# First mixture layer: where the unsplit fp32 rows of w2 come from, a load per buffer or a load per expert and a GpSimd copy per slot

## The chip, the cores and the metric

The kernel runs on one NeuronCore of a Trainium2 chip. The metric is the device time of one execution in microseconds. The median of three runs of the kernel before is 710.54 us (706.63 to 710.76). The execution that the profiler recorded took 707.83 us, of which 706.0 us are the span from its first to its last instruction.

## The reference

Attention with two kinds of window masks gives a matrix x of 2304 tokens by 512. Two mixture layers with 8 experts follow, and each token goes to one expert:

```
logits = x @ w_gate
e_idx = argmax(logits)
for e in range(8):
    h = relu(x[mask] @ w1[e])          # 512 x 1024
    ye = h @ w2[e]                     # 1024 x 512
    out[mask] = gate_w * eom * ye      # second layer: gate_w only
```

All arrays are fp32. An expert has 2 MB of w1 and 2 MB of w2.

## The kernel before

After the attention the tokens of each mixture layer are sorted by expert into slots of 128 rows, and the function `moe` works through the slots one after the other. In the first layer, the subject here, there are 23 slots (0 to 22) with these inputs. A slot is one pass of TensorE: 96 matmuls of 128 columns (L797) for x @ w1 in two halves of four hidden blocks, then 12 fp16 matmuls of 512 columns and 8 more, of which 4 are in fp32 (both L864), for h @ w2, and 12 small ones for the router of the next layer (L1017).

Weights are multiplied as a sum of two fp16 numbers, hi and lo. An expert's fp32 weights are loaded by DMA into `raw` (8 pieces of 128 x 1024, four of w1 and four of w2), ScalarE makes hi from them (L99) and VectorE makes lo (L104), both into one of two weight buffers, `wbuf[0]` and `wbuf[1]`, which alternate from slot to slot. The split is made anew for every slot. Its operations stand in strings: `B0:4` makes hi and lo of half pieces 0 to 4, `D0:4` loads the same half pieces of the slot after next into `raw`. The strings for a slot are `MO['ta1']`, which is `SQ4`; their four parts are issued at four places of the slot.

In this layer the last two pieces (half pieces 12 to 16, the last four blocks of w2) are not split: the last four matmuls of a slot multiply them in fp32 (`plain`, L77). `plains(s + 1)`, called at the start of slot s, loads these two pieces, 1 MB, by two DMAs straight into `wbuf[(s + 1) % 2]`.

SyncE (SP) issues all weight DMAs in order. Each is conditional: a register read from a table (`tab`, a value load, which is a TENSOR_LOAD and two register operations) says whether the expert of the slot is another one. `tab[:, 1]` says so against the slot before and steers the loads into `raw`; `tab[:, 2]` says so against the slot two before, which had the same buffer, and steers the loads into `wbuf`. With these inputs the experts have 3, 3, 2, 2, 3, 3, 4 and 3 slots, so the expert changes at slots 3, 6, 8, 10, 13, 16 and 20; the loads into `wbuf` move data for slots 3 and 4, 6 and 7, 8 and 9, 10 and 11, 13 and 14, 16 and 17, 20 and 21. In the other slots their instructions pass without moving data.

In a slot SP issues, in this order: `plains(s + 1)`; in slots 5 to 15 the loads of a part of the second layer's first expert (`Fill`, L930); two value loads; `D0:4`; the transpose of the last output rows for the router (`yT`, L1003) and their store (`y_dram`, L1004); the transposed gather of tokens (`xT`, L770); the other loads into `raw`. GpSimd (POOL) issues: the gather of tokens for slot s + 2 (L763); a copy of indices (L990); the lo part of the output rows (L998); in slots 6 to 16 the lo part of a fill (L940, L941).

Of the kernel before, what the change touches and what calls it, by code (L numbers as in the profile page):

```python
# [24 lines left out]
P = 128  # L25
# [12 lines left out]
SP4 = ['B0:4 D0:4', '', 'B4:6 D4:6', 'B6:8 D6:8 B8:12 D8:12 B12:14 D12:14 H14:16 L14:15 P15:16 D14:16']  # L38

UF = 12  # L40
SQ4 = ['B0:4 D0:4', '', 'B4:6 D4:6', 'B6:8 D6:8 B8:12 D8:12']
MO = {'ta1': SQ4, 'wm': 9, 'f': ['H0:2 H2:4 H4:6 H6:8 P0:2', 'L2:8', 'H14:16 H8:14 P14:16 L8:14'], 'rf': 18, 'yh': 1, 'ta': ['H0:4 L0:3 P3:4 D0:2', '', 'B4:6 D2:6', 'B6:8 D6:8 B8:12 D8:12 B12:14 D12:14 B14:16 D14:16'], 'tb': SP4,
      's3': ['B0:4 D0:4', 'B4:8 D4:8', 'B8:12 D8:12', ''], 's4': ['B0:4 D0:4', 'B4:8 D4:8', 'B8:12 D8:12 B12:14 D12:14 H14:16 L14:15 P15:16 D14:16']}
OOB = 1 << 20
ROW = 2 * DM + 16

# [2 lines left out]
def fused(ctx, tc, qk, vw, wr1, w1a, w2a, mid, wr2, mbias, w1b, w2b, cf, c16, cbs, cms, cib, out, dbg=None):  # L49
    nc = tc.nc  # L50
# [50 lines left out]
    def lo_piece(wb, k, n=2, pool=None):  # L101
        s = slice(k * 512, (k + n) * 512)
        if pool is None:
            nc.vector.scalar_tensor_tensor(out=wb[:, 1, s], in0=raw[:, s], scalar=SW, in1=wb[:, 0, s],  # L104
                                           op0=ALU.mult, op1=ALU.subtract)
        else:
            nc.gpsimd.tensor_scalar(pool[:, 0:n * 512], raw[:, s], SW, None, op0=ALU.mult)  # L107
            nc.gpsimd.tensor_tensor(wb[:, 1, s], pool[:, 0:n * 512], wb[:, 0, s], op=ALU.subtract)  # L108

    def splits(wb, ops, load=None):  # L110

        for o in ops.split():
# [478 lines left out]
    def sort(nm, lg, nt, inv, fe, ea, tab, scale, og, extra, gscale, start):  # L591
# [4 lines left out]
        T = work(nm, nt)  # L596
# [87 lines left out]
        v.tensor_scalar(sc, iota_t, nlast, -float(KA), op0=ALU.min, op1=ALU.add)  # L684
        cmp2 = T("cmp2", [NSLOT, E])
        v.tensor_tensor(cmp2, end.unsqueeze(1).to_broadcast([P, NSLOT, E]), sc.unsqueeze(2).to_broadcast([P, NSLOT, E]), op=ALU.is_le)
        ef = T("ef", [NSLOT + 2])
        v.memset(ef[:, 0:2], 0.0)
        v.tensor_reduce(out=ef[:, 2:], in_=cmp2, axis=AX.X, op=ALU.add)
        ei = T("ei", [NSLOT], I32)  # L690
        v.tensor_scalar(ei, ef[:, 2:], fe["g"], None, op0=ALU.add)
        v.tensor_tensor(tab[:, 1, 0:NSLOT], ef[:, 2:], ef[:, 1:NSLOT + 1], op=ALU.not_equal)
        v.tensor_tensor(tab[:, 2, 0:NSLOT], ef[:, 2:], ef[:, 0:NSLOT], op=ALU.not_equal)
        v.tensor_scalar(tab[:, 0, 0:NSLOT], ei, E - 1, None, op0=ALU.bitwise_and)
        eql = T("eql" + nm, [NSLOT])
        v.tensor_scalar(eql, iota_t, nlast, None, op0=ALU.is_equal)
# [520 lines left out]
```

## Time and profile before

| | |
|---|---|
| median of three runs | 710.54 us (706.63 to 710.76) |
| profiled execution | 707.83 us |
| its span | 706.0 us |
| mean granted TensorE clock | 0.946 of full speed |
| PE busy | 613.3 us (87%) |
| DVE busy | 523.3 us (74%) |
| ACT busy | 440.3 us (62%) |
| POOL busy | 394.5 us (56%) |
| moved by DMA | 133.72 MB |

PE is TensorE, DVE VectorE, ACT ScalarE. The attention takes about the first 160 us, the first mixture layer runs from 163.8 us to 468.5 us, the second to the end. The view of waits says who waited for whom, the timeline lists instructions with start, duration, and, in brackets, the idle time before them and what ended it. Times in all rows are microseconds from the start of the span, where not marked ns.

### The profile page before, as it was taken

What the parts mean: (1) busy time and instruction counts of PE and PEld (TensorE: products, weight loads), DVE (VectorE), ACT (ScalarE), POOL (GpSimd) and SP (SyncE); (2) the same over time, 40 slices, a digit from 0 to 9 for tenths busy, and PEclk for the clock granted to TensorE, in tenths of its full rate; (3) what the DMA queues carried; (4) which work ended last, traced back from release to release, by engine and by line L of the source; (5) the groups of instructions that cost most, each with busy time, mean ns of one, the idle gap of its engine ahead of it and who ended that gap; (6) DMA issues with size and microseconds to landing.
All of it is one profiled execution on the core that took longest, in us unless ns stands there. A gap on an engine that the chain in (4) does not pass through costs nothing. (4 is left out here: it accounts for less than half of the span.)

```text
span 706.0 us, 18711 instructions
## 1 busy us (share of the span) xinstructions
PE 613.3 (87%) x7180; PEld 458.7 (65%) x7180; DVE 523.3 (74%) x658; ACT 440.3 (62%) x529; POOL 394.5 (56%) x396
## 2 busy tenths in 40 slices
PE   3898879836989987999998979999799987999993
PEld 2788768725757664676675757676676764776771
DVE  4699887684349565686767845759399987999995
ACT  4687766531166556676757646731389866889883
POOL 2577675442472545576666832312679946756771
PEclk9999998857999998999999989999999998999997
DMA  9999999983687999998989589430953299323231
GB/s 203 231 228 241 244 242 251 266 239 90 163 232 164 301 238 275 339 252 263 274 244 253 133 209 259 103 65 17 291 85 105 77 306 289 58 68 92 61 78 47
DMA packets 134484, 133.72 MB, mean 189 GB/s; under 512 B 94447, under 2 KB 99311, under 8 KB 133360
## 3 DMA queue, kind: packets, MB, share of 16 engines
q1 hardware_dynamic: 128704, 114.56, 64.1%
q0 software_dynamic: 5280, 17.13, 8.2%
q8 instruction: 60, 0.98, 0.6%
q10 hardware_dynamic: 400, 0.72, 0.4%
q14 instruction: 40, 0.33, 0.1%
HBM read 209.91 MB, written 18.22 MB: 323 GB/s over the span
## 5 line engine op out<-in xcount | busy, mean ns | idle before, releaser
L104 DVE SCALAR_TENSOR_TENSOR wb<-raw,wb 128x1024 f16<-128x1024 f32 (+2 forms) x190 | 326.6, 1747 | 82.8 <-ACT wb L99 81.9
L99 ACT ACTIVATE wb<-raw 128x1024 f16<-128x1024 f32 (+1 forms) x190 | 256.9, 1399 | 69.1 <-DMA raw<-in_w1a 45.9
L797 PEld LDWEIGHTS <-wb 128*128 128x128 f16 x4032 | 232.8, 99 | 16.1 <-DMA xsA<-lotmp 6.7
L797 PE MATMUL ph<-xT,wb 128*128 128x128 f16 x3648 | 213.9, 221 | 3.7 <-DMA xT<-xg 3.7
L864 PE MATMUL py<-wb,hh 128*128 128x512 f16 x524 | 125.1, 392 | 16.0 <-ACT hh L808 16.0
L864 PE MATMUL py<-wb,hl 128*128 128x512 f32 (+1 forms) x304 | 112.4, 511 | 6.2 <-ACT hl L805 5.3
L864 PEld LDWEIGHTS <-hh 128*128 128x128 f16 x580 | 55.7, 100 | 79.7 <-ACT hh L808 17.4
L808 ACT ACTIVATE hh<-ph 128x512 f16<-128x512 f32 x61 | 36.3, 595 | 57.6 <-PE ph L797 39.6
L864 PEld LDWEIGHTS py<-wb,hl 128*128 128x128 f32 x168 | 32.9, 198 | 42.5 <-issue 32.3
L990 POOL COPY y<-idxaa 128x1 int32<-128x1 int32 x21 | 15.7, 745 | 74.2 <-DMA y_dram<-y 74.2
L107 POOL TENSOR_SCALAR lotmp<-raw 128x512 f32<-128x512 f32 x17 | 31.3, 1843 | 21.4 <-DMA raw<-in_w1b 20.1
L403 PE MATMUL po<-v,pT 128*96 128x65 f32 x384 | 41.4, 262 | 1.5 <-DMA v<-in_vw 1.5
L763 POOL DMA_INDIRECT xg<-x_dram,idxaa x23 | 37.4, 1628 | 8.3 <-DVE idxaa L669 4.2
L998 POOL TENSOR_TENSOR y<-y,y 128x512 f16<-128x512 f32 x21 | 31.9, 1519 | 17.5 <-ACT y L997 15.1
L108 POOL TENSOR_TENSOR wb<-lotmp,wb 128x512 f16<-128x512 f32 x17 | 29.6, 1743 | 18.3 <-issue 16.1
L403 PEld LDWEIGHTS po<-v,pT 128*96 128x96 f32 x384 | 38.2, 177 | 2.0 <-DMA v<-in_vw 1.6
L1109 POOL DMA_INDIRECT out<-y,idx x18 | 32.4, 1799 | 7.5 <-DMA raw<-in_w2b 4.7
L344 DVE TENSOR_REDUCE M<-ps 96x4 f32<-96x512 f32 x48 | 31.6, 678 | 3.4 <-PE ps L343 3.2
L301 DVE SCALAR_TENSOR_TENSOR kl<-qk,kh 128x608 f16<-128x608 f32 x32 | 29.2, 915 | 6.3 <-ACT kh L298 6.3
L809 DVE SCALAR_TENSOR_TENSOR hl<-ph,hh 128x512 f16<-128x512 f32 x38 | 25.7, 679 | 10.7 <-ACT hh L808 10.7
L342 PE MATMUL ps<-kh,qs 128*96 128x128 f16 x192 | 30.5, 234 | 3.0 <-ACT kh L298 2.9
L797 PE MATMUL ph<-xsA,wb 128*128 128x128 f16 x384 | 24.9, 229 | 8.2 <-DMA xsA<-lotmp 6.6
(358 smaller groups left out, 886.0 us busy)
## 6 DMA issues: line engine op xcount, KB each, us to landing
raw<-in_w1a SPq DMA_DIRECT2D x92, 512.0 KB
raw<-in_w1b SPq DMA_DIRECT2D x72, 512.0 KB
raw<-in_w2b SPq DMA_DIRECT2D x72, 512.0 KB
raw<-in_w2a SPq DMA_DIRECT2D x46, 512.0 KB
wb<-in_w2a SPq DMA_DIRECT2D x44, 512.0 KB
qk<-in_qk SPq DMA_DIRECT2D x16, 608.0 KB
v<-in_vw SPq DMA_DIRECT2D x16, 390.0 KB
y_dram<-y SPq DMA_DIRECT2D x21, 260.0 KB
```

Of the source, the lines that this page charges most:

```text
L99: nc.scalar.activation(wb[:, 0, s], raw[:, s], AF.Copy, scale=SW)
L104: nc.vector.scalar_tensor_tensor(out=wb[:, 1, s], in0=raw[:, s], scalar=SW, in1=wb[:, 0, s], op0=ALU.mult, op1=ALU.subtract)
L107: nc.gpsimd.tensor_scalar(pool[:, 0:n * 512], raw[:, s], SW, None, op0=ALU.mult)
L342: nc.tensor.matmul(ps[:, j, :], st, kh[:, h, QT * i:QT * i + 128], start=False, stop=False, skip_group_check=True)
L344: nc.vector.tensor_reduce(out=Ms[n][:, 4 * g:4 * g + 4], in_=ps, axis=AX.X, op=ALU.max)
L403: nc.tensor.matmul(po[:, i, :], pT[:, NQ * h + i, :], v[:, h, i, :], start=True, stop=True)
L763: nc.gpsimd.indirect_dma_start(t, None, src, bass.IndirectOffsetOnAxis(start.idx[:, s:s + 1], 0))
L797: nc.tensor.matmul(ph[:, j, :], w[:, c, fs], xT[:, parts[c + i], :], start=k == 0, stop=k == 47, skip_group_check=True)
L808: nc.scalar.activation(hs, ph, AF.Relu)
L864: nc.tensor.matmul(to, a, w, start=k == 0, stop=k == len(ops) - 1)
L998: gt.tensor_tensor(y16[:, DM:2 * DM], self.y, y16[:, 0:DM], op=ALU.subtract)
L1109: gt.indirect_dma_start(out, bass.IndirectOffsetOnAxis(idx2[:, s:s + 1] if s is not None else ilast, 0), y, None, bounds_check=N - 1, oob_ ...
```

## The change

The two unsplit pieces are now loaded into `raw`, as the other six are, by the same register as these: once for each expert. In every slot GpSimd copies them from there into the weight buffer of the next slot by two copies of 128 x 1024 fp32 (`C12:16`, issued behind `B8:12`). The third row of the table and its value load are gone.

```diff
-SQ4 = ['B0:4 D0:4', '', 'B4:6 D4:6', 'B6:8 D6:8 B8:12 D8:12']
+SQ4 = ['B0:4 D0:4', '', 'B4:6 D4:6', 'B6:8 D6:8 B8:12 C12:16 D8:12']
...
-      's3': ['B0:4 D0:4', 'B4:8 D4:8', 'B8:12 D8:12', ''], 's4': [...]}
+      's3': ['B0:4 D0:4', 'B4:8 D4:8', 'B8:12 D8:12', 'C12:16'], 's4': [...]}
...
+            if o[0] == "C":
+                for i in range(k // 2, e // 2):
+                    nc.gpsimd.tensor_copy(plain(wb)[i - UF // 2], raw[:, i * 1024:(i + 1) * 1024])
...
-        v.tensor_tensor(tab[:, 2, 0:NSLOT], ef[:, 2:], ef[:, 0:NSLOT], op=ALU.not_equal)
...
-            load_raw(w1, w2, regs[0], cond=regs[1], pieces=[k for k in pieces if k < npc])
+            load_raw(w1, w2, regs[0], cond=regs[1], pieces=[k for k in pieces if (k < npc) != rest])
...
         def plains(s):
 
-            if s < NSLOT and one:
-                c = None if s < KE + 2 else nc.sync.value_load(tab[0:1, 2, s:s + 1], min_val=0, max_val=1)
-                load_raw(w1, w2, evr.pop(s), cond=c, pieces=range(npc, 8), wb=wbuf[s % 2])
+            weights(s, always=s == KE, rest=True)
```

On POOL, in slot 7, the order before is this (`xg` is the gather, `idxaa` the table of token indices, `wb_2778` the buffer that the fill prepares for the second layer):

```order
L763 DMA xg_2779<-x_dram,idxaa 128x1024
L990 COPY y_2797<-idxaa 128x1
L998 TENSOR_TENSOR y_2797<-y_2801,y_2797 128x512
L940 TENSOR_SCALAR xgA_2783<-xgA_2783 128x512
L941 TENSOR_TENSOR wb_2778<-xgA_2783,wb_2778 128x512
```

and after the change:

```order
L766 DMA xg_2779<-x_dram,idxaa 128x1024
L990 COPY y_2797<-idxaa 128x1
L998 TENSOR_TENSOR y_2797<-y_2801,y_2797 128x512
L940 TENSOR_SCALAR xgA_2783<-xgA_2783 128x512
L941 TENSOR_TENSOR wb_2778<-xgA_2783,wb_2778 128x512
L123 COPY wb_69<-raw 128x1024 x2
```

The two copies come last in the slot, so they stand ahead of the gather, L990 and L998 of the next slot.

On SP, where slot 6 begins, the order before is this (`wb_2766` is `wbuf[1]`, the buffer of slot 7; the first row is the last load of `D8:12` of slot 5; `xgA` and `lotmp` are stages of the fill):

```order
L91 DMA raw<-in_w2a 128x2x512 [waits DMAHW6_49]
L786 TENSOR_LOAD tab_2787
L786 ISA x2
L91 ISA
L91 DMA wb_2766<-in_w2a 128x2x512 [waits DMAHW7_49,PE_49]
L91 ISA
L91 DMA wb_2766<-in_w2a 128x2x512 [waits DMAHW0_49,PE_49]
L930 ISA
L930 DMA xgA_2783<-in_w1b 128x512 [waits DMAHW1_49]
```

and after the change:

```order
L91 DMA raw<-in_w2a 128x2x512 [waits DMAHW6_49]
L91 ISA
L91 DMA raw<-in_w2a 128x2x512 [waits DMAHW7_49,Pool_49]
L91 ISA
L91 DMA raw<-in_w2a 128x2x512 [waits DMAHW0_49,Pool_49]
L930 ISA
L930 DMA xgA_2783<-in_w1b 128x512 [waits DMAHW1_49]
```

The value load is gone, the two loads have another target and another condition, and they wait for POOL (the copies of the slot before, which read `raw`) where they waited for PE.

## Rows read from the trace of the kernel before

**Rows 1.** Waits on all engines, 245 to 472 us: total, times, longest.
```profile
ACT wb L99 <- DMA raw<-in_w1a: 33.9, 10, 6.0
...
PE py L864 <- ACT hl L805: 5.3, 4, 2.2
PE py L864 <- ACT hh L808: 5.0, 4, 3.4
PE plg L1017 <- DMA yT<-y: 4.8, 2, 4.4
```

**Rows 2.** PE timeline, slots 7, 9, 10 and 11: start, duration, instruction.
```profile
266.56 4.45 PE L864 MATMUL py<-wb,hh 128*128 128x512 f16 x12 [3.38 <-ACT hh L808]
272.93 5.40 PE L864 MATMUL py<-wb,hl 128*128 128x512 f32 x8 [1.92 <-ACT hl L805]
...
299.12 3.70 PE L864 MATMUL py<-wb,hl 128*128 128x512 f32 x8 [0.85 <-ACT hl L805]
302.96 5.52 PE L797 MATMUL ph<-xT,wb 128*128 128x128 f16 x96
308.32 2.75 PE L864 MATMUL py<-wb,hh 128*128 128x512 f16 x12
310.91 3.60 PE L864 MATMUL py<-wb,hl 128*128 128x512 f32 x8
314.65 5.52 PE L797 MATMUL ph<-xT,wb 128*128 128x128 f16 x96
```

**Rows 3.** ACT timeline, slot 7.
```profile
261.75 1.91 ACT L99 ACTIVATE wb<-raw 128x2048 f16<-128x2048 f32 x1 [5.79 <-DMA raw<-in_w1a]
...
270.30 1.06 ACT L99 ACTIVATE wb<-raw 128x1024 f16<-128x1024 f32 x1 [3.79 <-DMA raw<-in_w1a]
```

**Rows 4.** SP timeline, slots 6, 8 and 11: the loads into wb and raw.
```profile
251.03 1.15 SPq L91 DMA_DIRECT2D wb<-in_w2a  x2
...
254.87 0.98 SPq L91 DMA_DIRECT2D raw<-in_w1a  x2
...
280.22 1.16 SPq L91 DMA_DIRECT2D wb<-in_w2a  x2
...
318.66 0.50 SPq L91 DMA_DIRECT2D wb<-in_w2a  x2
```

**Rows 5.** DMA rate, 250 to 260 us, in slices of 0.25 us.
```profile
GB/s 291 196 0 0 0 0 0 0 90 74 98 147 156 336 385 410 410 418 410 418 418 352 369 393 401 410 393 344 303 344 311 360 262 115 147 147 262 295 367 412
```

**Rows 6.** Line L786, the value load of the third table row: ns, minimum, median, maximum.
```profile
L786 SPq TENSOR_LOAD <-tab x19: 263/278/587, 221.8 to 457.2; - x19
```

**Rows 7.** POOL operations with one input: two casts (us, mean ns), and line L107 (ns).
```profile
L363 POOL CAST mb<-r 96x12 bf16<-96x12 f32 x16 | 3.0, 190 | 1.1
...
L499 POOL CAST identh<-cft 128x128 f16<-128x128 f32 x1 | 0.3, 290 | 0.0
...
L107 POOL TENSOR_SCALAR lotmp<-raw x17: 1487/1578/3439, 517.8 to 681.9; 128x512 f32<-128x512 f32 x17
```

**Rows 8.** Busy us of PE, PEld, DVE, ACT, POOL, then granted clock; sum over 251-390.
```profile
270.00:285.00 15.00, 13.08 (x125) 8.52 (x124) 10.04 (x8) 11.57 (x14) 9.52 (x6) 0.86 0.98 295
...
345.00:360.00 15.00, 15.00 (x142) 9.87 (x141) 12.08 (x11) 13.04 (x15) 13.72 (x8) 1.00 0.73 200
...
sum 139.00, PE 129.48 PEld 87.50 DVE 94.28 ACT 93.16 POOL 87.02; mean PE 14.39 PEld 9.72 DVE 10.47 ACT 10.35 POOL 9.67
```

**Rows 9.** DVE and POOL timelines, where the two overlap.
```profile
230.29 2.29 DVE L104 SCALAR_TENSOR_TENSOR wb<-raw,wb 128x2048 f16<-128x2048 f32 x1 [0.57 <-ACT wb L99]
...
230.40 2.30 POOL L180 TENSOR_SCALAR fe_ub<-fe_ob 128x8 f32<-128x8 f32 x1
...
308.92 2.37 POOL L940 TENSOR_SCALAR xgA<-xgA 128x512 f32<-128x512 f32 x1
...
310.30 1.23 DVE L104 SCALAR_TENSOR_TENSOR wb<-raw,wb 128x1024 f16<-128x1024 f32 x1 [0.36 <-ACT wb L99]
...
311.37 1.17 POOL L941 TENSOR_TENSOR wb<-xgA,wb 128x512 f16<-128x512 f32 x1
```

More of the change, by code (lines that the diff above doesn't have):

```diff
@@ L40 @@
 UF = 12
-SQ4 = ['B0:4 D0:4', '', 'B4:6 D4:6', 'B6:8 D6:8 B8:12 D8:12']
+SQ4 = ['B0:4 D0:4', '', 'B4:6 D4:6', 'B6:8 D6:8 B8:12 C12:16 D8:12']
 MO = {'ta1': SQ4, 'wm': 9, 'f': ['H0:2 H2:4 H4:6 H6:8 P0:2', 'L2:8', 'H14:16 H8:14 P14:16 L8:14'], 'rf': 18, 'yh': 1, 'ta': ['H0:4 L0:3 P3:4 D0:2', '', 'B4:6 D2:6', 'B6:8 D6:8 B8:12 D8:12 B12:14 D12:14 B14:16 D14:16'], 'tb': SP4,
-      's3': ['B0:4 D0:4', 'B4:8 D4:8', 'B8:12 D8:12', ''], 's4': ['B0:4 D0:4', 'B4:8 D4:8', 'B8:12 D8:12 B12:14 D12:14 H14:16 L14:15 P15:16 D14:16']}
+      's3': ['B0:4 D0:4', 'B4:8 D4:8', 'B8:12 D8:12', 'C12:16'], 's4': ['B0:4 D0:4', 'B4:8 D4:8', 'B8:12 D8:12 B12:14 D12:14 H14:16 L14:15 P15:16 D14:16']}
 OOB = 1 << 20
@@ L566, in fused @@
     xsb = [m1.tile([P, 8, P], F16, name=f"xT{i}") for i in range(3)]
-    tabs = [m1.tile([P, 3, 32], I32, name=f"tab{i}") for i in range(2)]
+    tabs = [m1.tile([P, 2, 32], I32, name=f"tab{i}") for i in range(2)]
     for t in tabs:
@@ L686, in sort @@
         v.tensor_tensor(cmp2, end.unsqueeze(1).to_broadcast([P, NSLOT, E]), sc.unsqueeze(2).to_broadcast([P, NSLOT, E]), op=ALU.is_le)
-        ef = T("ef", [NSLOT + 2])
-        v.memset(ef[:, 0:2], 0.0)
-        v.tensor_reduce(out=ef[:, 2:], in_=cmp2, axis=AX.X, op=ALU.add)
+        ef = T("ef", [NSLOT + 1])
+        v.memset(ef[:, 0:1], 0.0)
+        v.tensor_reduce(out=ef[:, 1:], in_=cmp2, axis=AX.X, op=ALU.add)
         ei = T("ei", [NSLOT], I32)
-        v.tensor_scalar(ei, ef[:, 2:], fe["g"], None, op0=ALU.add)
-        v.tensor_tensor(tab[:, 1, 0:NSLOT], ef[:, 2:], ef[:, 1:NSLOT + 1], op=ALU.not_equal)
-        v.tensor_tensor(tab[:, 2, 0:NSLOT], ef[:, 2:], ef[:, 0:NSLOT], op=ALU.not_equal)
+        v.tensor_scalar(ei, ef[:, 1:], fe["g"], None, op0=ALU.add)
+        v.tensor_tensor(tab[:, 1, 0:NSLOT], ef[:, 1:], ef[:, 0:NSLOT], op=ALU.not_equal)
         v.tensor_scalar(tab[:, 0, 0:NSLOT], ei, E - 1, None, op0=ALU.bitwise_and)
@@ L750, in moe @@
     def moe(w1, w2, tab, src, parts, post, start, wfirst):
-        xg, xs, regs, evr = {}, {i: xsA[i] for i in range(KA)}, [], {}
+        xg, xs, regs = {}, {i: xsA[i] for i in range(KA)}, []
         one = post is post1
@@ L772, in x_transpose, with weights @@
             post.gathered(s, g)
-        def weights(s, pieces=range(8), always=False):
+        def weights(s, pieces=range(8), always=False, rest=False):
             if s >= NSLOT:
@@ L779, in weights @@
                            None if always else nc.sync.value_load(tab[0:1, 1, s:s + 1], min_val=0, max_val=1), s)
-                evr[s] = regs[0]
-            load_raw(w1, w2, regs[0], cond=regs[1], pieces=[k for k in pieces if k < npc])
+            load_raw(w1, w2, regs[0], cond=regs[1], pieces=[k for k in pieces if (k < npc) != rest])
         def plains(s):
-            if s < NSLOT and one:
-                c = None if s < KE + 2 else nc.sync.value_load(tab[0:1, 2, s:s + 1], min_val=0, max_val=1)
-                load_raw(w1, w2, evr.pop(s), cond=c, pieces=range(npc, 8), wb=wbuf[s % 2])
+            weights(s, always=s == KE, rest=True)
         def mm1(g, w1h, w1l, xT, mid):
```

## The prediction, made before the changed kernel ran

> **What bounds the kernel now.** I read the view of waits first, then the PE timeline, then the queues behind its gaps. In the first mixture layer PE sets the pace: slot 10 begins at 302.96 and slot 11 at 314.65, so an undisturbed slot takes 11.69 us, and PE has no gap in it [rows 2]. What is lost stands beside this pace, and few waits carry it: between 245 and 472 us PE waits 5.0 us for hh, 5.3 us for hl and 4.8 us for yT, 15.1 us together [rows 1]. hh and hl are made by ScalarE, and ScalarE is not slow: in the same stretch it waits 33.9 us for the w1 pieces in `raw` [rows 1]. It works in order, so an hh that stands behind a split whose weights have not landed is late, and PE with it. The costliest place is slot 7: the split of slot 8's first pieces starts at 261.75 after 5.79 us of waiting, the next at 270.30 after 3.79 us [rows 3]; PE waits 3.38 us for hh and 1.92 us for hl, and its 12 and 8 matmuls take 4.45 and 5.40 us where slot 10 needs 2.75 and 3.60 [rows 2]. The granted clock of 270 to 285 us is 0.86, so part of the stretch ran at 1.2 instead of 2.4 GHz, after PE had stood idle [rows 8]. Slot 7 thus loses 5.30 us of waiting and 3.50 us of slow matmuls, 8.80 us. Slot 9 loses 0.85 us to hl [rows 2].
>
> The DMA queues cause this. The loads for slot 8 are issued at 254.87, and in front of them stand the 1 MB that `plains` loads into `wbuf` for slot 7, issued at 251.03 [rows 4], and two fills. From 253.5 to 256.5 us the rate is at 336 to 418 GB/s, about 400 [rows 5]: the queue is full, and what comes first delays what comes behind.
>
> **The change, part by part.**
>
> *Loads removed.* The expert changes at 7 slots. Before, each change moves 2 MB into the two buffers, now 1 MB into `raw`: 7 loads of 1 MB go, those for slots 4, 7, 9, 11, 14, 17 and 21. One takes 2 x 128 x 1024 x 4 B / 400 GB/s = 2.6 us of full queues, 18 us in all, but only what stands ahead of a late load counts.
> - The load for slot 7, at 251.03, stands ahead of the late one. Slot 8's pieces should land 2.6 us sooner, and the 3.38 us wait shrink to 0.8. The second wait, 1.92 us, is for the next piece, which shifts by as much; I leave it. Of the 1.70 us that the slow clock costs the 12 matmuls behind the first wait I take half, 0.85, since I can't tell whether 0.8 us of idling still lowers it. Bounds: 0 (the fills fill the gap) and 8.80 us. I take 3.45.
> - The load for slot 9, at 280.22 [rows 4], stands ahead of those for slot 10, which split late in slot 9: the 0.85 us wait should go. Bounds 0 and 0.85; I take 0.85.
> - The other five stand ahead of no late load of the same slot: the next expert comes three or more slots after each change, and its loads are issued a slot later, into queues that have drained. The waits that remain in [rows 1] after slots 7 and 9 (5.0 - 3.38, 5.3 - 1.92 - 0.85 and 4.8, together 8.95 us) belong to other slots. I take 0; bounds 0 and 8.95.
>
> *The value load.* SP saves one per slot, 0.28 us [rows 6], and pays three more in slot 2, where the register has been given to another slot in between. Below 1 us either way, off PE's path: 0.
>
> *Copies added.* Two copies of 128 x 1024 per slot on POOL, in 20 slots. The trace has no copy of this size. From the casts, 190 ns for 12 columns and 290 for 128 [rows 7], a column costs 0.86 ns, which makes 190 + 1012 x 0.86 = 1.06 us. From above, L107, also with one input, needs 1487 ns for 512 columns at the least [rows 7], so 2.97 us for 1024. I take 1.06, because the casts are the same kind of operation without arithmetic: 2.1 us per slot. POOL is busy 87.02 of 139 us, 7.3 us in 11.69 [rows 8], and 7.3 + 2.1 = 9.4 fits. What hides them: the buffer that they fill is read by the last four matmuls of the next slot, some 10 us later. They can't gain by themselves, since no instruction of POOL goes. I take 0; the price if the cover is gone is the slower rival below.
>
> *Waits added.* SP's loads at the start of a slot now wait for the copies of the slot before. Behind them on SP stand the fills, the loads of the next expert, yT, y_dram and xT; ScalarE and the router matmuls wait for these. In slot 10 the last fill operation on POOL ends at 311.37 + 1.17 = 312.54 [rows 9], the copies then at 314.7, and SP comes to that load at 318.66 [rows 4]: 4 us to spare. Behind the copies on POOL stand the gather, L990 and L998 of the next slot; SP's yT waits for L998. The gather is two slots ahead. I take 0.
>
> *VectorE against GpSimd.* At 230.40 an operation of 8 columns on POOL took 2.30 us, the length of the VectorE split that began at 230.29: it waited for it. But L940, on POOL from 308.92 to 311.29, did not keep the split at 310.30 from running its plain 1.23 us [rows 9]. So a copy may wait for a split of up to 2.29 us, and VectorE for less than a copy. VectorE is busy 94.28 of 139 us, 7.9 us per slot, and 7.9 + 2.1 is still under 11.69 [rows 8]; lo is made a slot ahead. 0.
> The Trainium skill ("SBUF — State Buffer", section "SBUF: two separate sides") calls the port pair of the two engines "an exclusive lock, not a bandwidth split", held for the whole instruction, also by a VectorE operation with two SBUF inputs. The first row agrees, the second does not. By that rule VectorE would lose the copies' full 2.1 us per slot, and in 345 to 360 us, where it is busy 12.08 of 15 us [rows 8], 9.4 + 2.1 = 11.5 us would leave it nothing to spare: the sum stays, the slower rival gains.
>
> *Sum.* 3.45 + 0.85 = 4.3 us. The profiled execution took 707.83 us, so 703.5. The median of the three runs is 2.7 us above the profiled execution; from it the same sum gives 706.2. I say 705.0, between the two.
>
> **Rivals.**
> 1. *Hidden anyway.* The fills and the transposes take the place of the removed megabyte, the pieces land when they did, and the copies cost nothing: 707.8 to 710.5, say 709. For it: in rows 5 the rate still reaches 412 GB/s at 260 us, long after the removed load. Against it: a queue in order must shorten by what leaves it. Chance 0.18.
> 2. *The whole of slot 7 goes.* SP itself is held by the full queues; if it runs ahead by 2.6 us the second piece is also issued sooner than it shifts, the clock stays up, and 8.80 + 0.85 us go, with half a microsecond at the yT wait of 4.4 us [rows 1]: 10.2 us, 697.6. For it: both waits have one cause. Against it: 3.79 us for the second piece is more than one megabyte. Chance 0.18.
> 3. *Slower: POOL becomes the bound.* A copy waits for a whole split, as the operation at 230.40 did, so 2 x (1.06 + 2.13) = 6.4 us per slot; at the price of L107 it is 5.9 without any wait. With 7.3 us of other work POOL needs 13.7 us, 2.0 over the slot's 11.69. It decides from 2.2 us per copy. L998, then yT and SP's loads come later from slot to slot. In the slots with fills that have no large wait of their own (8, 10 to 14 and 16, seven) this is 14 us, less the 4.3: 717.5. For it: POOL is busy 13.72 of 15 us from 345 to 360 us [rows 8]. Against it: much of that is itself waiting for VectorE. Chance 0.14.
>
> **How the numbers follow.** The forecast, 702 to 707, has a chance of 0.50. A measurement of this kernel tells about 1% (7 us) from no change. Faster by over 1% is rival 2 and a small part, 0.05, of the forecast: 0.23. Slower by over 1% is rival 3 but for 0.02 where POOL falls behind only a little: 0.12. Within 1%: 0.65. The range runs from 697, which takes in rival 2, to 715, which leaves out the bulk of rival 3: 697 to 715.
>
> **What would show it.** Right: in the profile after, `raw<-in_w2a` has as many issues as both targets had, with 7 MB less moved; slot 7's wait for hh is near 0.8 us; the copies take 1.1 us where VectorE is idle and up to 3.4 us behind a split; the undisturbed slots still take 11.69 us. Wrong: slots 10 to 14 get longer, SP waits for POOL at the loads into `raw`, or PE's wait in slot 7 is as long as before.

## The result and the profile after the change

The kernel got slower: 715.34 us median (712.37 to 718.13) against 709.39 us for the kernel before beside it, a ratio of 1.0092 with a 95% interval of 1.0062 to 1.0121. The prediction, 705.0 us, has the wrong sign, and the measured time lies 0.3 us above its range of 697 to 715. The profiled execution took 717.02 us, its span 715.2 us.

The page after the change: busy time of the engines, VectorE's split line and the copies.

```profile
PE 611.7 (86%) x7180; PEld 457.7 (64%) x7180; DVE 546.2 (76%) x656; ACT 440.0 (62%) x529; POOL 463.2 (65%) x438
...
L104 DVE SCALAR_TENSOR_TENSOR wb<-raw,wb 128x1024 f16<-128x1024 f32 (+2 forms) x190 | 349.2, 1870 | 69.0 <-ACT wb L99 64.2
...
L123 POOL COPY wb<-raw 128x1024 f32<-128x1024 f32 x42 | 72.0, 1735 | 16.4 <-DMA raw<-in_w2a 16.4
```

POOL has 72.0 us of copies, and VectorE 22.9 us more than the 523.3 us of before, though it was given no work. DMA moved 126.39 MB, the expected 7.3 MB less.

Where the time went is seen from slot lengths. I count a slot from one group of router matmuls to the next, and the layer from the first matmul of slot 0 to the group that ends slot 22 (one more group follows among the matmuls of the second layer):

```profile
167.29 2.95 PE L797 MATMUL ph<-xsA,wb 128*128 128x128 f16 x26 [6.65 <-DMA xsA<-lotmp]
...
478.13 0.45 PE L1017 MATMUL plg<-wr2h,yT 128*128 128x8 f16 x12
```

The layer (PE timeline, after) is 478.13 - 167.29 = 310.8 us long, against 468.5 - 163.8 = 304.7 before: 6.2 us. The other 3 us of the two profiled executions arise in the attention, which the change doesn't touch; over all the traces below the layer starts at 163.3 to 167.3. Slot lengths in us, for six kernels that are used below (slots not shown differ by less than 0.9, slot 8 by 1.2, slot 13 by 1.7, and slots 0 to 2 together by 1.6):

| slot | before | before again | after | before + constant copies | copies on ScalarE | no copies |
|---|---|---|---|---|---|---|
| 6 | 12.94 | 12.79 | 12.78 | 14.21 | 12.55 | 12.77 |
| 7 | 20.81 | 20.07 | 13.12 | 13.33 | 13.39 | 14.62 |
| 9 | 12.81 | 12.30 | 15.92 | 16.57 | 13.54 | 12.30 |
| 12 | 12.27 | 12.80 | 14.88 | 11.94 | 11.68 | 14.16 |
| 15 | 15.86 | 13.70 | 16.28 | 12.20 | 11.69 | 12.67 |
| 16 | 12.07 | 14.34 | 16.44 | 17.84 | 13.90 | 13.59 |
| 17 | 13.24 | 13.34 | 14.91 | 13.22 | 13.32 | 13.27 |
| 18 | 16.24 | 15.93 | 17.82 | 17.29 | 14.54 | 14.90 |
| layer | 304.7 | 304.5 | 310.8 | 307.6 | 295.8 | 297.2 |

Slot 7 lost what it was to lose, and more: 7.7 us. Slots 9, 12, 16, 17 and 18 gave back 13.3 us (11.3 against before again, whose slot 16 was longer by 2.3 without any change). The PE timeline of slots 7, 9, 12, 16 and of the router matmuls that end slots 17 and 18:

```profile
268.07 2.76 PE L864 MATMUL py<-wb,hh 128*128 128x512 f16 x12 [0.74 <-ACT hh L808]
271.11 2.38 PE L864 MATMUL py<-wb,hl 128*128 128x512 f32 x5 [0.28 <-ACT hl L805]
...
294.87 2.76 PE L864 MATMUL py<-wb,hh 128*128 128x512 f16 x12 [2.41 <-ACT hh L808]
299.04 3.24 PE L864 MATMUL py<-wb,hl 128*128 128x512 f32 x7 [1.41 <-ACT hl L805]
...
332.91 2.76 PE L864 MATMUL py<-wb,hh 128*128 128x512 f16 x12 [1.16 <-ACT hh L808]
337.29 3.67 PE L864 MATMUL py<-wb,hl 128*128 128x512 f32 x8 [1.62 <-ACT hl L805]
...
389.40 4.35 PE L864 MATMUL py<-wb,hh 128*128 128x512 f16 x12 [2.94 <-ACT hh L808]
...
411.93 0.46 PE L1017 MATMUL plg<-wr2h,yT 128*128 128x8 f16 x12 [2.11 <-DMA yT<-y]
...
429.75 0.46 PE L1017 MATMUL plg<-wr2h,yT 128*128 128x8 f16 x12 [4.34 <-DMA yT<-y]
```

In slot 7 the waits of [rows 2], 3.38 and 1.92 us, are 0.74 and 0.28, and the 12 matmuls take 2.76 us instead of 4.45: the clock stays up. In slots 9, 12 and 16 hh comes later than before, in 9 and 12 hl too. At the end of slot 17 yT comes late (2.11 us; 0.44 before), and the matmuls of slot 18 behind it are slower (PE busy 13.49 us instead of 11.86). The wait that ends slot 18 is not new, as this row of the kernel before shows:

```profile
419.61 0.48 PE L1017 MATMUL plg<-wr2h,yT 128*128 128x8 f16 x12 [4.38 <-DMA yT<-y]
```

The granted clock (third number from the end) of slot 7 before, and of slots 7, 9, 11 and 16 after the change; the columns are those of [rows 8]:

```profile
257.36:278.17 20.81, 15.52 (x130) 9.24 (x129) 9.53 (x8) 10.84 (x11) 9.05 (x6) 0.84 1.08 276
```
```profile
261.50:274.62 13.12, 12.11 (x130) 8.28 (x129) 10.73 (x7) 7.92 (x10) 12.88 (x8) 1.00 1.07 333
...
286.63:302.55 15.92, 12.10 (x129) 8.27 (x128) 8.82 (x7) 8.52 (x10) 13.76 (x10) 1.00 1.03 330
...
314.24:325.92 11.68, 11.68 (x130) 8.35 (x128) 11.68 (x8) 7.22 (x9) 11.52 (x7) 1.00 0.49 133
...
380.58:397.02 16.44, 13.50 (x132) 8.80 (x131) 13.58 (x15) 10.57 (x12) 13.39 (x11) 0.90 0.53 139
```

What makes those of slot 9 late is seen where slot 8 begins, at 274.62. First the timelines of DVE, POOL, SP and ACT after the change:

```profile
275.77 2.29 DVE L104 SCALAR_TENSOR_TENSOR wb<-raw,wb 128x2048 f16<-128x2048 f32 x1 [1.67 <-ACT wb L99]
278.06 3.05 DVE L104 SCALAR_TENSOR_TENSOR wb<-raw,wb 128x2048 f16<-128x2048 f32 x1
...
275.98 6.03 POOL L123 COPY wb<-raw 128x1024 f32<-128x1024 f32 x2 [0.85 <-DMA raw<-in_w2a]
...
278.95 3.16 SPq L91 DMA_DIRECT2D raw<-in_w2a  x4
284.80 0.97 SPq L91 DMA_DIRECT2D raw<-in_w1a  x2
...
291.18 1.91 ACT L99 ACTIVATE wb<-raw 128x2048 f16<-128x2048 f32 x1 [5.95 <-DMA raw<-in_w1a]
```

The two copies wait for their load, then take 6.03 us beside VectorE's splits, one of which takes 3.05 us instead of 2.29. SP stands at the four loads into `raw` until 282.1, when the copies have ended; the first loads for slot 10 follow at 284.80, and ScalarE gets their weights at 291.18. The kernel with the copies on ScalarE (below) shows the same place, its slot 8 beginning at 273.25:

```profile
277.15 1.30 SPq L91 DMA_DIRECT2D raw<-in_w2a  x4
282.16 0.97 SPq L91 DMA_DIRECT2D raw<-in_w1a  x2
...
274.52 1.99 ACT L123 ACTIVATE wb<-raw 128x1024 f32<-128x1024 f32 x2
287.93 1.91 ACT L99 ACTIVATE wb<-raw 128x2048 f16<-128x2048 f32 x1 [1.31 <-DMA raw<-in_w1a]
```

There the loads pass in 1.30 us, and the split starts 14.7 us after the slot's start, not 16.6. (The start of the same chain for slot 12 stands in the section on why the prediction was wrong; for slots 16 to 18 none is shown.) SP's waits after the change, 210 to 470 us (total, times, longest):

```profile
SPq L91 <- DVE wb L104: 16.8, 9, 3.3
SPq L1003 <- POOL wb L123: 12.6, 4, 7.3
SPq L91 <- POOL wb L123: 7.1, 3, 2.6
```

Before, SP had no wait for a copy, of course; it waited 13.2 us for DVE at L91.

### The profile page after: what moved, and what is told of

It is laid out like the page before. It is cut to its first block, busy times and chain, and to the rows that moved or that the text cites. A ratio compares the mean times of both kernels' runs of the same rounds, so it can differ in the third digit from the quotient of the medians.

```text
span 715.2 us, 18726 instructions
## 1 busy us (share of the span) xinstructions
PE 611.7 (86%) x7180; PEld 457.7 (64%) x7180; DVE 546.2 (76%) x656; ACT 440.0 (62%) x529; POOL 463.2 (65%) x438
## 2 busy tenths in 40 slices
DMA packets 130677, 126.39 MB, mean 177 GB/s; under 512 B 94223, under 2 KB 99087, under 8 KB 129552
## 5 line engine op out<-in xcount | busy, mean ns | idle before, releaser
L104 DVE SCALAR_TENSOR_TENSOR wb<-raw,wb 128x1024 f16<-128x1024 f32 (+2 forms) x190 | 349.2, 1870 | 69.0 <-ACT wb L99 64.2
L864 PE MATMUL py<-wb,hl 128*128 128x512 f32 (+1 forms) x304 | 109.1, 498 | 4.7 <-ACT hl L805 3.6
L123 POOL COPY wb<-raw 128x1024 f32<-128x1024 f32 x42 | 72.0, 1735 | 16.4 <-DMA raw<-in_w2a 16.4
L766 POOL DMA_INDIRECT xg<-x_dram,idxaa x23 | 39.3, 1709 | 8.3 <-DVE idxaa L673 4.2
L107 POOL TENSOR_SCALAR lotmp<-raw 128x512 f32<-128x512 f32 x17 | 30.6, 1797 | 20.9 <-DMA raw<-in_w1b 20.7
L407 PE MATMUL po<-v,pT 128*96 128x65 f32 x384 | 39.7, 255 | 1.5 <-DMA v<-in_vw 1.5
L998 POOL TENSOR_TENSOR y<-y,y 128x512 f16<-128x512 f32 x21 | 31.2, 1484 | 13.4 <-ACT y L997 8.6
L407 PEld LDWEIGHTS po<-v,pT 128*96 128x96 f32 x384 | 36.7, 171 | 1.9 <-DMA v<-in_vw 1.8
L396 ACT ACTIVATE pT<-pst 128x384 f32<-128x384 f32 x48 | 23.4, 487 | 16.3 <-PE pst L395 15.7
```

The costliest lines, as they stand in the source:

```text
L123: nc.gpsimd.tensor_copy(plain(wb)[i - UF // 2], raw[:, i * 1024:(i + 1) * 1024])
L407: nc.tensor.matmul(po[:, i, :], pT[:, NQ * h + i, :], v[:, h, i, :], start=True, stop=True)
L766: nc.gpsimd.indirect_dma_start(t, None, src, bass.IndirectOffsetOnAxis(start.idx[:, s:s + 1], 0))
L864: nc.tensor.matmul(to, a, w, start=k == 0, stop=k == len(ops) - 1)
L998: gt.tensor_tensor(y16[:, DM:2 * DM], self.y, y16[:, 0:DM], op=ALU.subtract)
```

## Experiments

Theory A, from the trace: the removed loads gain some 7 us, and the copies cost 13 to 14, mostly through waits that they bring into queues in order (GpSimd for the landing, SP for the copies). Rival B: through the time that GpSimd and VectorE take from each other. Where the last quarter of the weights is not copied, layer 2's routing differs; for those kernels (no copy, constant copies, one column, wait then copy, copy then wait) only the layer's length is compared, each time of one profiled execution. Behind the layer they take 247.6 to 252.6 us, where the kernel before takes 237.5, which I put down to the routing; so their totals (709.54, 725.01, 711.53, 729.35 and 723.60 us) say nothing on the copies, although the first two of them were expected as totals. Profiles of kernels that differ by a trifle give lengths within 3.5 us of each other (after: 310.8, 313.9, 310.5; before: 304.7, 304.5).

### What the loads give, what the waits cost

**No copy:** the C step does nothing, the rest is the changed kernel (here and in the next kernel a quarter of one buffer is zeroed once at the start).
```diff
-                    nc.gpsimd.tensor_copy(plain(wb)[i - UF // 2], raw[:, i * 1024:(i + 1) * 1024])
+                    pass
```


> The changed kernel without the GpSimd copies (the last four matmuls of a slot from slot 3 on then multiply zeros or what stands in the buffer). Theory A, the copies cost and the loads gain: the layer keeps slot 7's gain of some 7.7 us and loses the new waits of slots 9, 12, 16, 17 and 18, so 700 to 704 us, faster than before by 5 to 9 us, and VectorE's splits (L104) are back near 327 us. Theory B, the removed loads gain nothing and the gain of slot 7 in the profile of after is chance: within 2 us of before, 708 to 711.

Measured: layer 297.2, which is 7.4 us less than before. What was removed does gain. The value load of the third row (19 times 278 ns on SP) is gone here too, and no run parts it from the loads; SP's waits for PE at L91, which went with it, were 1.4 us before.

**One column:** the same waits, next to no copying.
```diff
-  nc.gpsimd.tensor_copy(plain(wb)[i - UF // 2], raw[:, i * 1024:(i + 1) * 1024])
+  nc.gpsimd.tensor_copy(plain(wb)[i - UF // 2][:, 0:1], raw[:, i * 1024:i * 1024 + 1])
```


> The changed kernel with copies of a single column of each piece, so that GpSimd still waits for the load, and SyncE for GpSimd, but the copy itself takes next to no time; the second product then reads weights that were not copied for the last quarter, so layer 2's routing differs and only layer 1 is compared. Theory A (waits): layer 1 304 to 308 long, with waits of PE for hh in slots 9, 12 and 16 of over 1 us as in the changed kernel. Rival B (time and lock): 297 to 300, as without copies.

Measured: layer 295.9. The copies of one column, 205 to 470 us:
```profile
L123 POOL COPY wb<-raw 128x1 f32<-128x1 f32 x42 | 33.2, 811 | 30.3 <-DMA raw<-in_w2a 23.0 <-PE py L866 7.3
```
GpSimd waits 23.0 us for the landing, more than in the changed kernel (16.4), and nothing is lost. Theory A falls in this form: the waits alone cost nothing that shows beside the scatter. VectorE's splits are longer here as well, by 65 ns (2413) and 189 ns (1526) in their two forms, 10 us in all, so that much lost time on VectorE is also without a price.

### What the time of the copies costs

**Constant copies:** source is a constant tile, so no wait for the load, and none of SP for the copy.
```diff
-  nc.gpsimd.tensor_copy(plain(wb)[i - UF // 2], raw[:, i * 1024:(i + 1) * 1024])
+  nc.gpsimd.tensor_copy(plain(wb)[i - UF // 2].rearrange("p (a b) -> p a b", b=128),
+                        identf.unsqueeze(1).to_broadcast([P, 8, 128]))
```


> The changed kernel with the copies reading a constant tile instead of raw (the last four matmuls then multiply constants): the same GpSimd work in the same place, but no copy waits for a load to land, and SP's loads don't wait for the copies. Theory A1, the cost comes through SP's wait for the copies and the copies' wait for the landing: most of it goes, 706 to 710 us. Theory A2, it comes through the time that the copies take on GpSimd and VectorE's queue (lock and order): 713 to 716 us, L104 still near 349 us, slot 16 still late.

Measured: layer 301.3, 4.0 more than without copies, hardly beyond the scatter.

**Before + constant copies:** the kernel before, all its loads kept, with these copies into the unused quarter of `raw`, in the same C steps.
```diff
+            if o[0] == "C":
+                for i in range(k // 2, e // 2):
+                    nc.gpsimd.tensor_copy(raw[:, i * 1024:(i + 1) * 1024].rearrange("p (a b) -> p a b", b=128),
+                                          identf.unsqueeze(1).to_broadcast([P, 8, 128]))
```


> The kernel before with its own loads, and on GpSimd, at the places where the changed kernel copies, two copies of the same size from a constant tile into the raw quarter that layer 1 does not use before: nothing waits for them and they wait for no load. Theory A (most of the loss comes through waits that the copies bring in, the copies' own time and the VectorE lock cost about 4 us, as between the layer lengths 297.24 and 301.28 of the two kernels with no copy and with constant copies): 711 to 714, layer 1 307 to 310 long. Rival B (the copies' time and lock cost all of it, some 13 us): 718 to 723, layer 1 over 314. The prediction's own step (copies hidden): 709, layer 1 304 to 306.

Measured: 714.37 us, ratio 1.0083 (1.0049 to 1.0117), 6 us, as much as the whole change. Copies that wait for nothing and that nothing waits for slow the kernel. That is about what theory A left for the copies' own time (711 to 714 us), and less than rival B needed (718 to 723). In the profile the layer is 307.6 us long, only 3 more than before; the 6 us rest on the times of whole executions.

**Wait then copy, copy then wait:** one column of each piece is read, before or behind full copies from the constant, so that either the copies stand behind the landing or SP behind the copies.
```diff
+  for i in range(k // 2, e // 2):
+      nc.gpsimd.tensor_copy(cdum[:, i:i + 1], raw[:, i * 1024:i * 1024 + 1])
   for i in range(k // 2, e // 2):
...
```
The loop left out is that of the constant copies; in the other kernel the added one stands behind it.


> The changed kernel; GpSimd first reads one column of both raw pieces (so it waits for their landing, and SyncE waits for these small reads), then copies from a constant tile into the buffer: the time of the copies stays, behind the landing, but SyncE is let go before it. The weights of the last quarter are a constant, so only layer 1 is compared. So far layer 1 is 297.2 long without copies, 295.9 with the waits but copies of one column, 301.3 with full copies that wait for nothing, 310.5 to 313.9 with both. If what makes both together dear is GpSimd, held by the copies that start only when the load has landed: 308 to 314. If it is SyncE, which waits for the copies' end: 299 to 303. Rival B (time and lock alone): 301 as with the constant copies.

> The other order: GpSimd copies from the constant tile as soon as it comes there, then reads one column of both raw pieces, for which SyncE waits: the copies don't wait for the load, but SyncE waits for their end. Only layer 1 is compared. GpSimd's part: 300 to 304; SyncE's part: 307 to 313; Rival B: 301.

Measured: 310.9 and 306.5. Copies behind the landing cost 9.6 us more than free ones and as much as the changed kernel's, even where SP is let go early. SP's wait for their end costs some 5 us. So a copy seems dearest when it begins at the landing of weights; the two shares don't add up. Each of the two kernels ran once, so neither has an interval; 5 and 9.6 us are beyond the 3.5 us of scatter, the first not by much.

### Its place in the queues

**Late load:** the copied pieces are loaded behind the slot's `xT`.
```diff
-                if s >= KE - 1:
-                    plains(s + 1)
...
             if s >= KA:
                 x_transpose(s + 2)
+            if one and s >= KE - 1:
+                plains(s + 1)
```


> The changed kernel with the loads of the copied pieces issued behind the slot's x transposes instead of ahead of them, so that SyncE's wait for the copies does not stand in front of the next expert's first loads. If that place in SyncE's queue is what costs most (A, SyncE's part): raw w1a loads of slots 10 and 13 again 5 to 7 us after the slot's start, waits for hh in slots 9 and 12 under 1 us, 708 to 712. If the landing of the load that GpSimd waits for matters more (A, GpSimd's part), the later load makes the copies later: 714 to 719. Rival B: unchanged, 713 to 717.

Measured: 727.12 us, ratio 1.0267 (1.0221 to 1.0312). A loss beyond what either way was expected to cost: GpSimd's copies wait 68.2 us for the landing (16.4 in the changed kernel), and SP waits 30.5 us at `yT` for the sum (L998 before) that stands behind them. The copies, 205 to 470 us:
```profile
L123 POOL COPY wb<-raw 128x1024 f32<-128x1024 f32 x38 | 55.7, 1492 | 70.7 <-DMA raw<-in_w2a 68.2 <-PE plg L1020 2.4
```

**Second layer's rank step early:** a step of the second layer's sorting goes ahead of slot 15's copies.
```diff
-    for s, k in ((15, 0), (15, 7), (16, 0), (16, 3), (16, 5), (16, 7), (17, 0), (17, 7)):
+    for s, k in ((15, 0), (15, 5), (16, 0), (16, 3), (16, 5), (16, 7), (17, 0), (17, 7)):
```


> The changed kernel with one step of the second layer's first sort (its rank step, in slot 15) issued before the copies of that slot instead of behind them. If slot 16's new wait of 2.94 us comes from that step standing on GpSimd behind two copies that wait for their load: the wait goes and 3 to 4 us with it, 711 to 712 us. If it comes from late loads like the others: no change, 714 to 716 us.

Measured: 713.59 us, 1.0080 (1.0047 to 1.0114), slot 16 is 16.78 us long: not this.

**Register kept:** the expert's number is kept, not read again, as in the late load above and the direct use below.
```diff
+                pair[s] = tuple(regs[:2])
...
-            weights(s, always=s == KE, rest=True)
+                ev, c = pair.pop(s)
+                load_raw(w1, w2, ev, cond=c, pieces=range(npc, 8))
```


> Control for the kernels that keep the expert's number in a register: the changed kernel with that alone, two value loads per slot fewer on SyncE. All theories: 713 to 717, layer 1 309 to 312 long, the same waits for hh in slots 9, 12 and 16. It is also a second profile of the changed kernel's layer 1, for its scatter.

Measured: 714.10 us, 1.0082 (1.0052 to 1.0111), layer 313.9, slots 12 and 16 long again (16.31, 16.55); slot 9 only 13.18. From 205 to 478 us the trace has 40 value loads of the table instead of 42, not two fewer per slot, so this is the changed kernel in all but that, measured again.

### Copies on other engines

**ScalarE** (two measurements):
```diff
-  nc.gpsimd.tensor_copy(plain(wb)[i - UF // 2], raw[:, i * 1024:(i + 1) * 1024])
+  nc.scalar.activation(plain(wb)[i - UF // 2], raw[:, i * 1024:(i + 1) * 1024], AF.Copy)
```


> The changed kernel with the copies on ScalarE instead of GpSimd: the same loads, the same waits for the landing and of SyncE for the copy, but no GpSimd time and no lock against VectorE, and 2 copies more per slot on the engine that makes the high parts and hh. Theory A (GpSimd's occupied time, drawn out by VectorE's splits, is what the waits multiply): 704 to 710, layer 1 300 to 306. Rival B2 (any copy that stands behind the landing in an in-order engine costs this, on whichever engine): 713 to 720.

> Both copies on ScalarE, timed in five rounds beside the two others: 696 to 700, layer 1 294 to 299, if the first measurement holds; 703 to 708 if it was luck.

Measured: 697.38 and 698.09 us, 0.9844 (0.9790 to 0.9899) and 0.9897 (0.9858 to 0.9935); layer 295.8 and 294.0. This is 7 to 11 us less than before. Against the changed kernel (714.1 to 715.3, ratios of 1.0080 to 1.0092) it is 16 to 18 us less by the medians; by the ratios, each against the kernel before beside it, 13 to 18. Both ways expected for the first measurement were too high.

**ScalarE, GpSimd held:** behind the copies on ScalarE, GpSimd reads a column of the result.
```diff
+  for i in range(k // 2, e // 2):
+      nc.gpsimd.tensor_copy(cdum[:, i:i + 1], plain(wb)[i - UF // 2][:, 0:1])
```


> The copies on ScalarE, and on GpSimd behind them two reads of one column of what was copied, at the place where the changed kernel copies: GpSimd's queue is held until the copies have ended, but does none of the copying. Output complete. If the held queue (sums, gathers behind it) is what the copies on GpSimd cost: 705 to 714, layer 1 303 to 311. If it is the time that GpSimd and VectorE take from each other while both work: 696 to 701, layer 1 295 to 298.

Measured: 699.38 us, 0.9843 (0.9779 to 0.9907), layer 298.5. GpSimd is held 68.4 us, longer than by the landing in the changed kernel, and little is lost (0 to 2 us, where the interval is 9 us wide). The reads, 205 to 470 us:
```profile
L125 POOL COPY cdum<-wb 128x1 f32<-128x1 f32 x42 | 34.0, 839 | 68.4 <-ACT wb L123 68.4
```

**VectorE**, and **VectorE, GpSimd held** (the same with that read):
```diff
-  nc.gpsimd.tensor_copy(plain(wb)[i - UF // 2], raw[:, i * 1024:(i + 1) * 1024])
+  nc.vector.tensor_copy(plain(wb)[i - UF // 2], raw[:, i * 1024:(i + 1) * 1024])
```


> The copies on VectorE, in its own order, with the landing waited for there; GpSimd's queue is as in the kernel before. Output complete. If VectorE's time is what counts (it loses 24 us in layer 1 in the changed kernel by longer splits): 20 slots x 2 copies of about 0.6 to 1.1 us are 24 to 44 us more on VectorE, so 708 to 720, layer 1 305 to 316. If GpSimd's held queue is what counts: 697 to 703, layer 1 296 to 300.

> The copies on VectorE, and on GpSimd, where the changed kernel copies, two reads of one column of what was copied: VectorE loses the copies' 29 us, GpSimd's queue is held until they have ended, and GpSimd does none of the copying. Output complete. If the two latenesses together are what the copies on GpSimd cost: 708 to 715, layer 1 305 to 311. If it is that the two engines keep each other waiting while both work: 700 to 705, layer 1 297 to 302.

Measured: 701.71 us, 0.9906 (0.9866 to 0.9946), and 706.76 us, 0.9984 (0.9949 to 1.0020); layers 299.2 and 302.0. The held queue costs 5 us here: GpSimd waits 91.2 us for VectorE's copies. The second time lies between the two that were expected for it.

**Second copy on ScalarE:** the first on GpSimd, or, in the other kernel, by `nc.vector` on VectorE.
```diff
-  for i in range(k // 2, e // 2):
-      nc.gpsimd.tensor_copy(plain(wb)[i - UF // 2], raw[:, i * 1024:(i + 1) * 1024])
+  nc.gpsimd.tensor_copy(plain(wb)[0], raw[:, 6144:7168])
+  nc.scalar.activation(plain(wb)[1], raw[:, 7168:8192], AF.Copy)
```


> The first copy of a slot on GpSimd, the second on ScalarE. If each copy on GpSimd costs its share: midway between 698 (both on ScalarE) and 714.5 (both on GpSimd), 704 to 708, layer 1 301 to 306. If only the pair, back to back, does harm: 697 to 702, layer 1 296 to 299. If the first GpSimd instruction behind the landing does it all: 710 to 715.

> The first copy on VectorE (0.73 us), the second on ScalarE (1.05 us), none on GpSimd. If GpSimd is what matters: 696 to 702, layer 1 295 to 299, like the kernels with both on ScalarE (297 to 299 measured 697.4 and 699.4) and both on VectorE (701.7). If any copy that VectorE's splits stand behind costs: 702 to 708.

Measured: 703.15 us, 0.9956 (0.9933 to 0.9979), and 699.97 us, 0.9898 (0.9849 to 0.9948). Beside each other, one copy on GpSimd costs 4 to 5 us over both on ScalarE (698.09), where two cost 13 to 18. The first time lies just under what a share per copy was to give. The layers in the profiles, 297.6 and 299.5 us, don't show the difference.

VectorE's two forms of split and the copies, 205 to 470 us (count, busy us, mean ns): first before, then after, copies on ScalarE, copies on VectorE, and before with constant copies. The last row has the shortest, the middle and the longest of all copies after the change, in ns.

```profile
L104 DVE SCALAR_TENSOR_TENSOR wb<-raw,wb 128x2048 f16<-128x2048 f32 x41 | 96.2, 2348 | 31.2 <-ACT wb L99 30.5 <-ACTq L880 0.6
L104 DVE SCALAR_TENSOR_TENSOR wb<-raw,wb 128x1024 f16<-128x1024 f32 x40 | 53.4, 1337 | 30.3 <-ACT wb L99 30.1
```
```profile
L104 DVE SCALAR_TENSOR_TENSOR wb<-raw,wb 128x2048 f16<-128x2048 f32 x41 | 111.0, 2709 | 34.0 <-ACT wb L99 29.9 <-issue 4.0
L123 POOL COPY wb<-raw 128x1024 f32<-128x1024 f32 x40 | 68.9, 1745 | 16.4 <-DMA raw<-in_w2a 16.4
L104 DVE SCALAR_TENSOR_TENSOR wb<-raw,wb 128x1024 f16<-128x1024 f32 x38 | 59.5, 1575 | 14.7 <-ACT wb L99 14.7
```
```profile
L104 DVE SCALAR_TENSOR_TENSOR wb<-raw,wb 128x2048 f16<-128x2048 f32 x42 | 98.7, 2350 | 42.3 <-ACT wb L99 42.2
L104 DVE SCALAR_TENSOR_TENSOR wb<-raw,wb 128x1024 f16<-128x1024 f32 x40 | 57.4, 1436 | 19.2 <-ACT wb L99 19.0
L123 ACT ACTIVATE wb<-raw 128x1024 f32<-128x1024 f32 x42 | 42.2, 1048 | 1.8 <-DMA raw<-in_w2a 1.7
```
```profile
L104 DVE SCALAR_TENSOR_TENSOR wb<-raw,wb 128x2048 f16<-128x2048 f32 x41 | 99.4, 2424 | 20.9 <-ACT wb L99 20.3 <-ACTq L880 0.6
L123 DVE COPY wb<-raw 128x1024 f32<-128x1024 f32 x42 | 28.8, 726 | 0.0
```
```profile
L104 DVE SCALAR_TENSOR_TENSOR wb<-raw,wb 128x2048 f16<-128x2048 f32 x41 | 103.2, 2516 | 31.9 <-ACT wb L99 31.8
L122 POOL COPY raw<-cft 128x1024 f32<-128x1024 f32 x42 | 68.4, 1656 | 0.0
L104 DVE SCALAR_TENSOR_TENSOR wb<-raw,wb 128x1024 f16<-128x1024 f32 x40 | 63.4, 1592 | 18.5 <-ACT wb L99 18.3
```
```profile
L123 POOL COPY wb<-raw x42: 1026/1040/3105, 211.1 to 471.4; 128x1024 f32<-128x1024 f32 x42
```

On GpSimd each copy takes 1745 ns where it takes 1048 on ScalarE and 726 on VectorE, and VectorE's splits pay too: 361 ns on each of 41 and 238 on each of 38, 24 us. The mean of GpSimd's copies hides two cases: 25 of the 42 take 1.03 or 1.04 us, and 17 take 2.0 to 3.1, all of these beside a split. With the copies on ScalarE the big splits take 2350 ns, as before, and the small ones 1436, 99 more. And GpSimd's constant copies, which stand behind no landing, lengthen the splits by 168 and 255 ns, 17 us in all.

### No copy at all

**Direct use:** the last four matmuls of a slot read `raw`, and the pieces of a new expert are loaded at the start of the slot that uses them first.
```diff
-                if s >= KE - 1:
-                    plains(s + 1)
+                if s >= KE:
+                    plains(s)
...
-                wf = [t.rearrange("p (f d) -> p f d", d=DM) for t in plain(wb)]
+                src = plain(wb) if s < KE else [raw[:, i * 1024:(i + 1) * 1024] for i in range(npc, 8)]
+                wf = [t.rearrange("p (f d) -> p f d", d=DM) for t in src]
```


> No copies: TensorE reads the unsplit pieces from raw itself, and they are loaded once per expert at the start of the slot that uses them first, after the last matmul of the slot before. The output is complete. Theory A: 700 to 705 us, if the pieces land before the last four matmuls, some 8 us after the issue. Rival: they land late where the queues are full (7 changes, 2 to 4 us each), 710 to 725 us, with PE waiting for raw<-in_w2a at L864.

Measured: 701.17 us, 0.9876 (0.9840 to 0.9913), also less than before and after. In the profile, of an execution of 703.29 us, the layer is 299.5 us long, with slots 7 and 9 at 17.48 and 17.94.

**Before again:** the kernel before without an edit.

> The kernel before, profiled once more, since its slot 7 (20.81 us long, with 5.3 us of waits and a clock of 0.84) is what the removed loads were to mend, and slot 7 was 13.33 us long in the kernel before with constant copies, which has all its loads. If slot 7's wait comes from the doubled loads: 20 to 21.5 us again, layer 1 304 to 306. If it is one execution's chance, 12 to 17 and layer 1 some 4 us shorter or with another slot long in its place.

Measured: slot 7 is 20.07 us long, layer 304.5. It is not one execution's chance. But before + constant copies has all its loads and a slot 7 of 13.33: there slots 6 and 9 are longer, and slots 6 to 9 together take 56.9 us, as in before again (56.8; first profile 58.2). After the change they take 53.8, with copies on ScalarE 52.4, with copies of one column 54.0, without copies 51.4.

## Why the prediction was wrong

*Loads removed: right in sign, too small.* I took 3.45 us for slot 7 and 0.85 for slot 9. Slot 7 gained 7.7, by what rival 2 named: both waits went and the clock stayed up. The wait for hh is 0.74 us, the 0.8 that I worked out; the second wait, which I had left, went with it. Slot 9 gained nothing, and lost 3.1. Yet one slot is the wrong unit, since the stall also moves when nothing is removed. Over slots 6 to 9 the loads are worth 3 to 7 us (58.2 and 56.8 against 51.4 without copies and 54.0 with one column), over the layer 7.4, and 7 to 11 us of the total where the copies cost nothing. So the term was mis-sized: 4.3 taken, 7 to 11 measured; the other changes of expert, taken at 0, carry some of it (slots 12, 15 and 18 with copies on ScalarE).

*Copies added: the price was right, the 0 was wrong.* There were 21 pairs of copies, not 20. A copy alone takes 1.04 us (1.06 worked out), and the longest 3.1 (up to 3.4 expected), on the average 1.74 us; and with them the other engine's splits grow. This is the step that failed: "What hides them: the buffer that they fill is read by the last four matmuls of the next slot, some 10 us later. [...] I take 0." The reader of the copy does have 10 us; VectorE, and what stands behind the copies on GpSimd and SP, don't. The constant copies, which keep nothing waiting but these, cost 6 us; the copies of the change, which also begin at the landing, 13 to 18.

*VectorE against GpSimd: the 0 was wrong.* I summed busy time, 7.9 + 2.1 under 11.69. VectorE had the time on average, but not everywhere: in slots 11 and 14 after the change it is busy from end to end (11.68 of 11.68 us, 11.69 of 11.69). When new weights land, ScalarE, VectorE and the copies all start on them, and the next loads into `raw` wait for their end. I had also let L940, beside which a split ran its plain time, stand for the copies. It doesn't: the split that begins at 278.06 inside a copy takes 3.05 us instead of 2.29. Why the two differ no run shows.
The measured loss is 24 us in 20 slots, 1.2 us per slot. The Trainium skill ("SBUF — State Buffer", section "SBUF: two separate sides") lets GpSimd and a VectorE operation with two SBUF inputs, as the splits are, exclude each other for a whole instruction, and leaves ScalarE out of it. The trace agrees on ScalarE (big splits of 2350 ns, as before) and in kind on the pair; the full 2.1 us per slot for VectorE that I worked out from the rule is more than the 1.2 measured.

*Waits added: the "4 us to spare" of slot 10 were not there.* I had its copies end at 314.7 and SP come to its loads at 318.66. POOL and SP timelines after the change, slot 10's copies and the loads that wait for them:

```profile
314.60 6.14 POOL L123 COPY wb<-raw 128x1024 f32<-128x1024 f32 x2
...
316.84 4.01 SPq L91 DMA_DIRECT2D raw<-in_w2a  x4
```

The copies began at 314.60, behind L941, when I had them end, and took 6.14 us, to 320.7; SP stood until 320.85, and with it the loads for slot 13. As a cost of its own this wait is small (one-column copies lose nothing, ScalarE's neither); it passes on the time by which GpSimd is late.

*Rival 3 had the sign and nearly the size (717.5), not the mechanism.* Its price per pair, 6.4 us, is that of the pairs at 275.98 and 314.60 (6.03 and 6.14), but the mean is 3.5 us per slot, since more than half of the copies wait for no split. POOL didn't become the bound; the busy times of [rows 8] after the change, sum over 251 to 390 us:

```profile
sum 139.00, PE 124.80 PEld 87.13 DVE 108.02 ACT 90.58 POOL 125.16; mean PE 124.80 PEld 87.13 DVE 108.02 ACT 90.58 POOL 125.16
```

125.16 us of 139 are 10.5 us in a slot of 11.69, and slots 10, 11 and 14 still take 11.69 us. The time is lost in slots 9, 12 and 16 to 18. So four of my signs of being right came true (as many issues, 7 MB less; 0.74 us for hh; 1.04 and 3.1 us for the copies; slots of 11.69 us) in a kernel that got slower; of the signs of being wrong, SP's 7.1 us for POOL at the loads into `raw` came, and slot 12 got longer.

*The account.* With the loads gone and copies that cost little: 697 to 698 us (copies on ScalarE). GpSimd as their place: 13 to 18 more, by the ratios. Of this, GpSimd held and VectorE busier, both without copying on GpSimd, make 6 to 10 us (0.9984 against 0.9844 and 0.9897); each alone makes 0 to 4. The rest, some 7 us (0.9984 against 1.0080 to 1.0092), is found by difference alone; I put it down to the two engines holding each other up, which the rows show but no run prices by itself. How that rest divides between later loads, later splits and later `yT` isn't settled: each edit that undid one of them also moved the copies in time.

## What to carry to other kernels

Don't price an added operation by its own reader's slack: ask what else stands in the engine's queue, which engine it excludes, and at what moment it becomes ready; an operation that waits for a load becomes ready just when all others for that load do. Before giving work to the least busy engine, try it on one that doesn't contend with the critical one: ScalarE, busier than GpSimd before, took the copies at no price that shows (layer 295.8 and 294.0 us, 297.2 without copies). And take a stall's worth over the stretch in which it can move, not from the slot where a profile shows it.

## What the hardware showed unexpectedly

- A 128 x 1024 fp32 copy takes 726 ns on VectorE, 1048 on ScalarE, and on GpSimd 1.04 us in 25 of 42 cases, but up to 3.1, with a mean of 1745 ns, where VectorE's splits run beside it. A copy of one column on GpSimd took 811 ns on average and 184 in the middle case.
- Copies on GpSimd that wait for nothing and feed nothing cost 6 us of 708 (3.5 to 8.3 by the interval), as much as the whole change.
- Waiting and the slow clock behind it don't go together in every slot. In slot 7 before, 5.30 us of waiting went with a loss of 8.80, at a granted clock of 0.84; the 1.02 us left after the change cost no clock. But slot 9 after the change waits 2.41 us for hh and 1.41 for hl at a granted clock of 1.00, and its 12 matmuls take 2.76 us, while slot 16 waits 2.94 us for hh, at 0.90, and its 12 take 4.35.
